# A new hand-written order for the opening of a gated-recurrence and MLP kernel, from the first unit's logarithms to the second product stage

## The chip, the cores and the metric

The kernel runs on one core of a Trainium2 chip. The metric is the time of one execution on the device, in microseconds (us). Lower is better. TensorE (PE, with its weight loads PEld), VectorE (DVE), ScalarE (ACT), GpSimd (POOL) and SyncE (SP) each run their own instructions in order, and meet through semaphores.

## The reference, cut to what matters

A linear attention with a complex, elementwise gate (4 batches, 8 heads, 768 positions, head width 48) feeds a two-layer MLP with ELU (384 to 2048 to 384). All inputs of the attention are float32; the weights arrive in the kernel as float64 bit patterns that it turns to float32 itself.

```python
mag = np.sqrt(a_re * a_re + a_im * a_im)
scale = np.minimum(mag, 0.999) / (mag + 1e-06)
a_re_n, a_im_n = (a_re * scale, a_im * scale)
for t in range(S):                      # S = 768
    ar, ai = (a_re_n[:, :, t, :, None], a_im_n[:, :, t, :, None])
    new_re = ar * S_re - ai * S_im
    new_im = ar * S_im + ai * S_re
    kv = np.einsum('bhd,bhe->bhde', k[:, :, t], v[:, :, t])
    S_re, S_im = (new_re + kv, new_im)
    y[:, :, t] = np.einsum('bhd,bhde->bhe', q[:, :, t], S_re)
...
x = y.transpose(0, 2, 1, 3).reshape(B * S, H * D)
h = x @ w_in
g = np.where(h > 0.0, h, np.exp(np.minimum(h, 0.0)) - 1.0)
return g @ w_out
```

## The kernel before, in words

The work is cut into 12 units. A unit is 128 positions of two batches, so 256 rows of the MLP. Within a unit the recurrence is done in closed form: the logarithm of the gate's size and its angle are summed over the positions by matmuls with triangular masks, and q and k are multiplied by the resulting decays and waves, so that attention becomes matmuls of "gated" q and k with a carried state.

One unit's chain, with the names of the code and the lines of the profile, is as follows.

- `squares` and `joined` (L709, L710 on ACT, L716 on DVE), and for unit 0, in smaller pieces, `squared` and `joined` (L720 on PE); then `logarithms` (L731 for unit 0, L735 and L736 later) and `powers` (L742 for unit 0, L746 and L747 later) on ACT.
- `lengths` (L766, L772), `ratios` (L757, L759, L760) and `slopes` (L780) on DVE, then `angles` (L811, L815) on ACT, an arctangent. From unit 2 on, `carried` (L826, DVE) adds the angle carried over from an earlier unit.
- `noted` (L791, ACT) notes whether the inputs lie where the fast way holds.
- `sums`, `summed`, `decayed` and `decays` (L872, L879, L920, L932, L889, L904): sums of logarithms on PE and their exponentials on ACT. `ends` (L946 to L954) takes the last of them for the state.
- `turned` and `turns` (L837 on PE, L842, L845, L849 on DVE): sums of angles, reduced to one turn. `carry_on` (L862) sends the last row on to a later unit. `waves` (L973, L976, L977, ACT): sine and cosine.
- `scaled` (L982, L986, L992) and `gated` (L1003): products of q and k with decays and waves, on DVE.
- `transposed` (L1023 on PE, L1024 a copy on ACT), `scores` (L1031, L1036) or `scored` (L1136, L1145), `states` (L1064, L1077, L1079, L1081), `values` or `valued` (L1100, L1109, with copies L1121 and L1126), and `seam` (L1190), a DMA that brings the rows of the attention into the places where the MLP reads them.

The MLP of units 0 and 1 consists of 16 `inner` and 16 `project` pieces for both units together. An `inner` (L1210) computes two blocks of 128 hidden columns for 256 rows in a PSUM bank; its `elu` uses ACT twice (L1219, L1220) and DVE once (L1221); a `project` (L1235) multiplies four such blocks by the second weight. From unit 2 on, the second layer uses sums of weight blocks (`combined`, `summed_in`, `folded`, and `product`, L1319), and from unit 3 on both layers do (L1455).

The weights come in 16 chunks, eight of each weight: `fetch` (L644) issues a chunk's DMA on SP, and `convert` does the next of the five DVE operations (L40, L43, L46, L50, L655) that make float32 of it. `load_a`, `load_qk` and `load_v` (L598) issue a unit's inputs on SP too. `warm` (L1557) issues small matmuls whose result nobody reads. `table` (L1200) loads ACT's table of functions ahead of its use. [...]three named w for the attention, three named mlp for inner products, warm matmuls and some accumulators, and y0 and y1.

The order of the opening is written by hand: the list `first` holds pieces, each with its arguments, and each engine gets its share of them in the order of the list. Units 0, 1 and 2 and the start of unit 3 are in the list. What is not in it comes from a plan of slots (`put`), sorted by time, and follows the list:

```python
items = [(fn, tuple(args)) for fn, *args in first]
items += [x[2:] for x in sorted(plan, key=lambda x: x[:2]) if x[2:] not in items]
for fn, args in items:
    fn(*args)
```

A piece moved in the list moves on every engine that it uses, and on the DMA queue.

Of the kernel before, what the change touches and what calls it, by code (L numbers as in the profile page):

```python
# [505 lines left out]
def kernel(  # L506
# [999 lines left out]
    def pronounced():  # L1506
# [13 lines left out]
        out=ident, in_=ident, pattern=[[-1, C]], base=0, channel_multiplier=1,  # L1520
# [57 lines left out]
    def gates_of(u, *at):  # L1578
# [5 lines left out]
    first = [  # L1584
        (warm, 1), (warm, 12), (fetch, "in", 0), (begun, 0), (inverses, 0), (inverses, 1),
        (load_qk, 0), (squared, "ar", 0), (load_v, 0), (squared, "ar", 1), (squared, "ai", 0),
        (joined, 0, 0), (squared, "ai", 1), (joined, 0, 1), (logarithms, 0, 0),
        (logarithms, 0, 1), (fetch, "in", 1), (fetch, "in", 2), (ratios, 0, 0), (lengths, 0, 0),
        (warm, 2), (warm, 1), (lengths, 0, 1), (sums, 1), *2 * [(convert,)],
        (table, "exp_and_others"), (ratios, 0, 1), (powers, 0, 0), (powers, 0, 1), (warm, 2),  # L1590
        (sums, 0), (warm, 1), (angles, 0, 0), (angles, 0, 1), (summed, 0), (summed, 1),
        (decayed, 0, 0), (turned, 0, 0), (decayed, 0, 1), (turned, 0, 1), (waves, 0, 0),
        (waves, 0, 1), (begun, 1), (warm, 1), (scaled, 0, "q", 0), (ends, 0), (scaled, 0, "k", 0),
        (scaled, 0, "k", 1), (scaled, 0, "q", 1), (warm, 1), (gated, 0, 0), (warm, 1), (noted, 0),
        (table, "natural_log"), (warm, 2), (gated, 0, 1), (warm, 2), *3 * [(convert,)],
        (transposed, 0, "k", 0), (transposed, 0, "q", 1), (carry_on, 0), (transposed, 0, "q", 0),
        *4 * [(convert,)], (scores, 0, 0), (transposed, 0, "k", 1), (scores, 0, 1), (load_a, 1),
        (squares, 1), (joined, 1), (fetch, "in", 3), (logarithms, 1), (states, 0, 0),
        (values, 0, 0), (powers, 1), (convert,), (states, 0, 1), (lengths, 1), (load_qk, 1),
        (convert,), (ratios, 1), (values, 0, 1), (seam, 0), (warm, 2), (warm, 2), (decays, 1),  # L1600
        (load_a, 2), (warm, 1), (inner, 0, 0), *2 * [(convert,)], (noted, 1), (scaled, 1),
        (warm, 4), (convert,), (load_v, 1), (slopes, 1), (ends, 1), *3 * [(convert,)],
        (inner, 0, 2), (elu, 0, 0), (convert,), (fetch, "in", 4), (angles, 1), (turns, 1),
        (waves, 1), (gated, 1, 0), (inner, 0, 4), (gated, 1, 1), (transposed, 1, "q", 0),
        (transposed, 1, "k", 0), (convert,), (scores, 1, 0), (load_v, 2), (convert,),
        (fetch, "in", 5), *2 * [(convert,)], (transposed, 1, "k", 1), (states, 1, 0), (convert,),
        (inner, 0, 6), (fetch, "in", 6), (elu, 0, 2), *4 * [(convert,)], (transposed, 1, "q", 1),
        (scores, 1, 1), (fetch, "in", 7), (values, 1, 0), (states, 1, 1), (values, 1, 1),
        (convert,), (seam, 1), *4 * [(convert,)], (inner, 0, 8), (inner, 0, 10), (elu, 0, 4),
        *2 * [(convert,)], (elu, 0, 6), (elu, 0, 8), (fetch, "out", 0), (warm, 2), (inner, 1, 0),  # L1610
        (convert,), (inner, 0, 12), (convert,), (inner, 1, 2), *3 * [(convert,)], (inner, 1, 4),
        (fetch, "out", 1), (fetch, "out", 2), (fetch, "out", 3), (elu, 0, 10), (convert,),
        (inner, 0, 14), (elu, 1, 0), *3 * [(convert,)], (elu, 0, 12), (fetch, "out", 4),
        *3 * [(convert,)], (elu, 1, 2), (inner, 1, 6), *2 * [(convert,)], (fetch, "out", 5),
        (elu, 1, 4), *3 * [(convert,)], (elu, 0, 14), *3 * [(convert,)], (elu, 1, 6),
        (begun, 2), (squares, 2), *2 * [(convert,)], (inner, 1, 8), (inner, 1, 10), (joined, 2),
        (convert,), (inner, 1, 12), (fetch, "out", 6), (fetch, "out", 7), *2 * [(convert,)],
        (elu, 1, 8), (convert,), (project, 0, 0, 0, 4), (convert,), (elu, 1, 10),
        *3 * [(convert,)], (elu, 1, 12), (load_qk, 2), *4 * [(convert,)], (inner, 1, 14),
        (elu, 1, 14), (logarithms, 2), (powers, 2), *4 * [(convert,)], (project, 1, 0, 0, 4),  # L1620
        (project, 1, 1, 0, 4), *3 * [(convert,)], (noted, 2), (lengths, 2), (ratios, 2),
        (slopes, 2), (load_a, 3), (angles, 2), (carried, 2), (convert,), (project, 0, 1, 0, 4),
        (convert,), (project, 0, 0, 4, 8), *3 * [(convert,)], (decays, 2), (project, 1, 0, 4, 8),
        *2 * [(convert,)], (project, 1, 1, 4, 8), (turns, 2), *2 * [(convert,)],
        (project, 0, 1, 4, 8), (begun, 3), (squares, 3), *2 * [(convert,)],
        (project, 1, 0, 8, 12), (waves, 2), (scaled, 2), (joined, 3), (gated, 2), (ends, 2),
        (load_qk, 3), (logarithms, 3), (powers, 3), (project, 1, 1, 8, 12),
        (states, 2, 0), (project, 1, 0, 12, 16), (transposed, 2, "q", 0), (lengths, 3),
        (ratios, 3), (project, 0, 0, 8, 12), (transposed, 2, "k", 0), (transposed, 2, "q", 1),
        (slopes, 3), (angles, 3), (project, 1, 1, 12, 16), (transposed, 2, "k", 1),  # L1630
        (carried, 3), (scored, 2), (turns, 3), (project, 0, 1, 8, 12), (valued, 2), (seam, 2),
        (noted, 3), (project, 0, 0, 12, 16), (opened,), (waves, 3), (summed_in, 0),
        (summed_in, 1), (combined, 1, 0), (combined, 2, 0), (summed_in, 2), (combined, 1, 1),
        (combined, 4, 0), (combined, 2, 1), (scaled, 3), (combined, 4, 1), (ends, 3),
        (project, 0, 1, 12, 16),
    ]
    def layer_of(u, at_h, at_p):
        if u == PAIRED:
# [129 lines left out]
```

## Time and profile before

| what | value |
|---|---|
| times of three runs | 670.13, 671.49, 674.26 us (median 671.49) |
| the profiled execution | 669.23 us, of which the span of the trace is 667.1 us |
| PE busy | 639.6 us (96%), weight loads 579.6 us (87%) |
| DVE busy | 503.6 us (75%) |
| ACT busy | 419.2 us (63%) |
| POOL busy | 154.4 us (23%) |
| HBM | 48.91 MB read, 4.80 MB written |

Busy time is what the profiler records between start and end of an instruction, without register, branch, semaphore and DMA-issuing instructions. "PEclk" is the clock that the throttle granted to PE, as a share of full speed. A line such as L1210 is a line of the kernel; where a wait is named, the arrow stands before the instruction that ended it.

### The profile page before, as it was taken

The numbers are of one execution on the slowest core, as the hardware profiler recorded it, in microseconds if no ns is written. First come the engines' busy times: TensorE is split into PE (matmuls) and PEld (weight loads), VectorE is DVE, ScalarE is ACT, GpSimd is POOL, SyncE is SP. The second block draws the span as 40 slices with busy tenths as digits, with TensorE's granted clock in tenths as the row PEclk, the third lists the DMA queues.
The fourth block names the chain that finished last, engine by engine and source line by source line (L and its number), as shares of the span: only waits on it lengthen the run. The fifth ranks groups of instructions, "written<-read, shape, count | busy, mean of one in ns | idle before, by whom it ended". The sixth has DMA issues, their size and how long they took to land.

```text
span 667.1 us, 17231 instructions
## 1 busy us (share of the span) xinstructions
PE 639.6 (96%) x7236; PEld 579.6 (87%) x7236; DVE 503.6 (75%) x801; ACT 419.2 (63%) x684; POOL 154.4 (23%) x200
## 2 busy tenths in 40 slices
PE   8899899999999899999999999999999999999995
PEld 6777786576898798998998998999999999999995
DVE  5889999968777788678678768768768768765481
ACT  6885455874846567667677677677677577471250
POOL 2000000112124303503503503503603602402000
PEclk9799999999999999999999999999999999999999
DMA  9986645630900632452451451451551551212100
GB/s 166 189 142 105 148 149 167 112 72 20 154 3 15 115 56 62 81 106 57 86 106 53 90 104 48 97 104 44 100 104 44 102 104 43 54 32 61 34 2 29
DMA packets 151443, 56.12 MB, mean 84 GB/s; under 512 B 129684, under 2 KB 143164, under 8 KB 151356
## 3 DMA queue, kind: packets, MB, share of 16 engines
q1 hardware_dynamic: 147616, 53.58, 38.8%
q0 software_dynamic: 3520, 1.20, 1.5%
q8 instruction: 59, 0.97, 0.6%
q14 instruction: 28, 0.23, 0.1%
q10 hardware_dynamic: 220, 0.14, 0.1%
HBM read 48.91 MB, written 4.80 MB: 81 GB/s over the span
## 4 chain that ended last, share of the span: by engine, by line
PE 44%; DVE 10%; ACT 8%; issue 3%; DMA 1%; SPq 0%; ACTq 0%; DVEq 0%
PE mlp L1319 18%; PE mlp L1455 10%; PE y L1455 5%; DVE g L1471 3%; PE w L1023 3%; DVE g L1480 3%; PE y L1109 2%; ACT ee L1477 2%; ACT ee L1476 2%; PE w L1064 2%; PE w L837 2%; DVE g L1297 1%; ACT L735 1%; DVE n L772 1%; ACT n L746 1%
## 5 line engine op out<-in xcount | busy, mean ns | idle before, releaser
L1319 PE MATMUL mlp<-w_out,g 128*128 128x192 f32 x640 | 111.8, 328 | 1.0 <-DVE ee L1331 1.0
L1319 PEld LDWEIGHTS mlp<-w_out,g 128*128 128x128 f32 x640 | 104.2, 190 | 4.4 <-DVE ee L1331 1.6
L1081 POOL TENSOR_TENSOR S<-S,T 128x384 f32<-128x384 f32 x36 | 30.9, 857 | 175.5 <-DVE S L1079 175.5
L1210 PE MATMUL mlp<-x,w_in 128*128 128x256 f32 x288 | 65.1, 381 | 3.0 <-DVE g L1221 2.6
L1210 PEld LDWEIGHTS mlp<-x,w_in 128*128 128x128 f32 x288 | 53.8, 190 | 11.7 <-DVE g L1221 3.1
L1471 DVE TENSOR_TENSOR g<-g,mlp 128x512 f32<-128x512 f32 x45 | 30.7, 682 | 40.1 <-ACT qt L1024 28.7
L1297 DVE TENSOR_TENSOR g<-g 128x512 f32<-128x512 f32 x80 | 54.4, 695 | 5.0 <-PE mlp L1319 3.8
L1455 PE MATMUL mlp<-x,w_in 128*128 128x128 f32 x424 | 56.2, 275 | 0.4 <-DVE o L1344 0.4
L1480 DVE SCALAR_TENSOR_TENSOR g<-ee,g 128x512 f32<-128x512 f32 x63 | 47.6, 755 | 11.1 <-ACT ee L1477 11.0
L1319 PE MATMUL mlp<-w,g 128*128 128x192 f32 x320 | 54.5, 329 | 0.0
L1319 PEld LDWEIGHTS mlp<-w,g 128*128 128x128 f32 x320 | 51.8, 190 | 0.6
L1455 PEld LDWEIGHTS mlp<-x,w_in 128*128 128x128 f32 x424 | 51.6, 192 | 0.8 <-DVE o L1344 0.6
L1476 ACT ACTIVATE ee<-g 128x512 f32<-128x512 f32 x63 | 39.5, 627 | 17.2 <-DVE g L1471 16.7
L1190 POOL DMA_DIRECT2D x<-y x62 | 29.8, 488 | 87.2 <-ACT y L1126 37.3
L1468 ACT COPY g<-mlp 128x512 f32<-128x512 f32 x36 | 21.1, 586 | 44.0 <-PE mlp L1455 43.7
L1477 ACT ACTIVATE ee<-ee 128x512 f32<-128x512 f32 x72 | 45.4, 631 | 2.3
L1024 ACT COPY qt<-w 128x512 f32<-128x512 f32 x48 | 25.8, 589 | 15.5 <-PE w L1023 15.4
L973 ACT ACTIVATE cs<-n 128x768 f32<-128x768 f32 (+1 forms) x14 | 10.5, 751 | 38.0 <-DVE n L845 37.9
L904 ACT ACTIVATE n<-w 64x384 f32<-64x384 f32 (+1 forms) x60 | 28.1, 486 | 8.9 <-PE w L889 8.3
L1455 PE MATMUL mlp<-x,g 128*128 128x128 f32 x224 | 29.7, 275 | 1.2 <-DVE o L1344 1.2
L1219 ACT ACTIVATE ee<-mlp 128x512 f32<-128x512 f32 x24 | 14.3, 595 | 25.6 <-PE mlp L1210 17.2
L1455 PE MATMUL y<-x,w_in 128*128 128x128 f32 x216 | 29.0, 277 | 1.4 <-ACT g L1468 1.4
(222 smaller groups left out, 1434.8 us busy)
## 6 DMA issues: line engine op xcount, KB each, us to landing
w<-in_moe_w_out_dram SPq DMA_DIRECT2D x8, 768.0 KB
g<-in_moe_w_in_dram SPq DMA_DIRECT2D x24, 256.0 KB
g<-in_moe_w_out_dram SPq DMA_DIRECT2D x24, 256.0 KB
w<-in_moe_w_in_dram SPq DMA_DIRECT2D x16, 288.0 KB
vn<-in_v_dram SPq DMA_DIRECT2D x24, 192.0 KB
ar<-in_a_re_dram SPq DMA_DIRECT2D x22, 192.0 KB
ai<-in_a_im_dram SPq DMA_DIRECT2D x22, 192.0 KB
q<-in_q_dram SPq DMA_DIRECT2D x22, 192.0 KB
```

Source lines behind the costliest of these rows:

```text
L904: nc.scalar.activation(out=flat(x[key][to, n : n + 1]), in_=t[of], func=AF.Exp, scale=sign)
L1024: nc.scalar.copy(out=o[:, h0 : h0 + 4], in_=t)
L1081: eng.tensor_tensor(out=new_s, in0=new_s, in1=wide, op=ALU.mult)
L1190: eng.dma_start(out=x["x"][ds(j * HP + D, G), i], in_=x["y"][ds(j * HP + i * G, G)])
L1210: nc.tensor.matmul(t[:, e], lhsT=w_in[:, i, ts(f + e, C)], rhs=x["x"][:, i], start=(i == 0), stop=(i == NI - 1),)
L1297: nc.vector.tensor_tensor(out=S_of(u, k, h), in0=a, in1=b, op=op)
L1319: nc.tensor.matmul(to, lhsT=a[:, m], rhs=b[:, m], start=(first and h == 0 and m == 0), stop=False, skip_group_check=True,)
L1455: nc.tensor.matmul(x["c" + c][:, ts(m, C)], lhsT=a[:, m], rhs=x["mix"][p], start=(p == BANKS[c][0] and m == 0), stop=False, skip_group_che ...
L1471: nc.vector.tensor_tensor(out=part(u, to), in0=part(u, a), in1=part(u, b), op=op)
L1476: nc.scalar.activation(out=e, in_=part(u, of), func=AF.Relu, scale=-1.0)
L1477: nc.scalar.activation(out=e, in_=e, func=AF.Exp, scale=-1.0)
L1480: nc.vector.scalar_tensor_tensor(out=part(u, to), in0=nat[u]["e", to], scalar=-1.0, in1=part(u, of), op0=ALU.add, op1=ALU.max,)
```

## The change

Only the list `first` changes. From the first unit's logarithms on it is written in another order:

- The first conversion of weights goes between unit 0's own operations, five steps in all, instead of two steps before and three after its gates. The table load for logarithms moves in between unit 0's transposes.
- The loads are permuted: `load_a(1)` goes ahead of `fetch` of chunk "in" 2, `load_qk(1)` ahead of chunk "in" 3, `load_a(3)` ahead of `load_qk(2)`, and `load_a(4)` is placed by the list, ahead of `load_v(3)`.
- Unit 0's states go ahead of its scores, its values behind them.
- Unit 1's chain (`decays`, `slopes`, `angles`, `turns`, `ends`, `scaled`) goes ahead of the first two inner pieces, (0,0) and (0,2), and unit 1's transposes, scores and states follow them. The inner pieces, their elus and the conversions after that are permuted: (0,6) ahead of (0,4), (1,8) and (0,14) ahead of (0,12) and (1,6).
- Unit 2's chain is spread among the conversions, and projects (1,0,8 to 12), (1,1,12 to 16) and (0,0,12 to 16) change places with others.
- Unit 3's `turns` goes behind the first combined sums of weights, its gates for q and for k are placed one by one, and the list goes on into unit 2's first five inner pieces and unit 4's `begun` and `squares`.
- The tables of the sine are loaded by an explicit piece for units 1, 2 and 3. The counts of warm matmuls change.

```diff
@@ -1584,55 +1584,62 @@
     first = [
         (warm, 1), (warm, 12), (fetch, "in", 0), (begun, 0), (inverses, 0), (inverses, 1),
         (load_qk, 0), (squared, "ar", 0), (load_v, 0), (squared, "ar", 1), (squared, "ai", 0),
-        (joined, 0, 0), (squared, "ai", 1), (joined, 0, 1), (logarithms, 0, 0),
-        (logarithms, 0, 1), (fetch, "in", 1), (fetch, "in", 2), (ratios, 0, 0), (lengths, 0, 0),
-        (warm, 2), (warm, 1), (lengths, 0, 1), (sums, 1), *2 * [(convert,)],
-        (table, "exp_and_others"), (ratios, 0, 1), (powers, 0, 0), (powers, 0, 1), (warm, 2),
-        (sums, 0), (warm, 1), (angles, 0, 0), (angles, 0, 1), (summed, 0), (summed, 1),
-        (decayed, 0, 0), (turned, 0, 0), (decayed, 0, 1), (turned, 0, 1), (waves, 0, 0),
-        (waves, 0, 1), (begun, 1), (warm, 1), (scaled, 0, "q", 0), (ends, 0), (scaled, 0, "k", 0),
-        (scaled, 0, "k", 1), (scaled, 0, "q", 1), (warm, 1), (gated, 0, 0), (warm, 1), (noted, 0),
-        (table, "natural_log"), (warm, 2), (gated, 0, 1), (warm, 2), *3 * [(convert,)],
-        (transposed, 0, "k", 0), (transposed, 0, "q", 1), (carry_on, 0), (transposed, 0, "q", 0),
-        *4 * [(convert,)], (scores, 0, 0), (transposed, 0, "k", 1), (scores, 0, 1), (load_a, 1),
-        (squares, 1), (joined, 1), (fetch, "in", 3), (logarithms, 1), (states, 0, 0),
-        (values, 0, 0), (powers, 1), (convert,), (states, 0, 1), (lengths, 1), (load_qk, 1),
-        (convert,), (ratios, 1), (values, 0, 1), (seam, 0), (warm, 2), (warm, 2), (decays, 1),
-        (load_a, 2), (warm, 1), (inner, 0, 0), *2 * [(convert,)], (noted, 1), (scaled, 1),
-        (warm, 4), (convert,), (load_v, 1), (slopes, 1), (ends, 1), *3 * [(convert,)],
-        (inner, 0, 2), (elu, 0, 0), (convert,), (fetch, "in", 4), (angles, 1), (turns, 1),
-        (waves, 1), (gated, 1, 0), (inner, 0, 4), (gated, 1, 1), (transposed, 1, "q", 0),
-        (transposed, 1, "k", 0), (convert,), (scores, 1, 0), (load_v, 2), (convert,),
-        (fetch, "in", 5), *2 * [(convert,)], (transposed, 1, "k", 1), (states, 1, 0), (convert,),
-        (inner, 0, 6), (fetch, "in", 6), (elu, 0, 2), *4 * [(convert,)], (transposed, 1, "q", 1),
-        (scores, 1, 1), (fetch, "in", 7), (values, 1, 0), (states, 1, 1), (values, 1, 1),
-        (convert,), (seam, 1), *4 * [(convert,)], (inner, 0, 8), (inner, 0, 10), (elu, 0, 4),
-        *2 * [(convert,)], (elu, 0, 6), (elu, 0, 8), (fetch, "out", 0), (warm, 2), (inner, 1, 0),
-        (convert,), (inner, 0, 12), (convert,), (inner, 1, 2), *3 * [(convert,)], (inner, 1, 4),
-        (fetch, "out", 1), (fetch, "out", 2), (fetch, "out", 3), (elu, 0, 10), (convert,),
-        (inner, 0, 14), (elu, 1, 0), *3 * [(convert,)], (elu, 0, 12), (fetch, "out", 4),
-        *3 * [(convert,)], (elu, 1, 2), (inner, 1, 6), *2 * [(convert,)], (fetch, "out", 5),
-        (elu, 1, 4), *3 * [(convert,)], (elu, 0, 14), *3 * [(convert,)], (elu, 1, 6),
-        (begun, 2), (squares, 2), *2 * [(convert,)], (inner, 1, 8), (inner, 1, 10), (joined, 2),
-        (convert,), (inner, 1, 12), (fetch, "out", 6), (fetch, "out", 7), *2 * [(convert,)],
-        (elu, 1, 8), (convert,), (project, 0, 0, 0, 4), (convert,), (elu, 1, 10),
-        *3 * [(convert,)], (elu, 1, 12), (load_qk, 2), *4 * [(convert,)], (inner, 1, 14),
-        (elu, 1, 14), (logarithms, 2), (powers, 2), *4 * [(convert,)], (project, 1, 0, 0, 4),
-        (project, 1, 1, 0, 4), *3 * [(convert,)], (noted, 2), (lengths, 2), (ratios, 2),
-        (slopes, 2), (load_a, 3), (angles, 2), (carried, 2), (convert,), (project, 0, 1, 0, 4),
-        (convert,), (project, 0, 0, 4, 8), *3 * [(convert,)], (decays, 2), (project, 1, 0, 4, 8),
-        *2 * [(convert,)], (project, 1, 1, 4, 8), (turns, 2), *2 * [(convert,)],
-        (project, 0, 1, 4, 8), (begun, 3), (squares, 3), *2 * [(convert,)],
-        (project, 1, 0, 8, 12), (waves, 2), (scaled, 2), (joined, 3), (gated, 2), (ends, 2),
-        (load_qk, 3), (logarithms, 3), (powers, 3), (project, 1, 1, 8, 12),
-        (states, 2, 0), (project, 1, 0, 12, 16), (transposed, 2, "q", 0), (lengths, 3),
-        (ratios, 3), (project, 0, 0, 8, 12), (transposed, 2, "k", 0), (transposed, 2, "q", 1),
-        (slopes, 3), (angles, 3), (project, 1, 1, 12, 16), (transposed, 2, "k", 1),
-        (carried, 3), (scored, 2), (turns, 3), (project, 0, 1, 8, 12), (valued, 2), (seam, 2),
-        (noted, 3), (project, 0, 0, 12, 16), (opened,), (waves, 3), (summed_in, 0),
-        (summed_in, 1), (combined, 1, 0), (combined, 2, 0), (summed_in, 2), (combined, 1, 1),
-        (combined, 4, 0), (combined, 2, 1), (scaled, 3), (combined, 4, 1), (ends, 3),
-        (project, 0, 1, 12, 16),
+        (joined, 0, 0), (squared, "ai", 1), (joined, 0, 1), (logarithms, 0, 0), (logarithms, 0, 1),
+        (fetch, "in", 1), (ratios, 0, 0), (warm, 2), (lengths, 0, 0), (convert,), (sums, 0),
+        (lengths, 0, 1), (sums, 1), (convert,), (ratios, 0, 1), (warm, 1),
+        (table, "exp_and_others"), (warm, 2), (powers, 0, 0), (powers, 0, 1), (summed, 0),
+        (convert,), (angles, 0, 0), (angles, 0, 1), (convert,), (summed, 1), (decayed, 0, 0),
+        (convert,), (turned, 0, 0), (turned, 0, 1), (decayed, 0, 1), (warm, 1), (warm, 1),
+        (begun, 1), (scaled, 0, "q", 0), (scaled, 0, "k", 1), (scaled, 0, "k", 0), (ends, 0),
+        (waves, 0, 0), (waves, 0, 1), (scaled, 0, "q", 1), (gated, 0, 0), (warm, 1), (noted, 0),
+        (warm, 1), (load_a, 1), (gated, 0, 1), (fetch, "in", 2), (transposed, 0, "q", 0),
+        (carry_on, 0), (transposed, 0, "k", 0), (table, "natural_log"), (convert,),
+        (transposed, 0, "q", 1), *2 * [(convert,)], (squares, 1), (convert,), (states, 0, 0),
+        (scores, 0, 0), (transposed, 0, "k", 1), (joined, 1), (load_qk, 1), (fetch, "in", 3),
+        (logarithms, 1), (convert,), (warm, 2), (convert,), (powers, 1), (states, 0, 1), (warm, 2),
+        (lengths, 1), (values, 0, 0), (scores, 0, 1), (warm, 2), (ratios, 1), (decays, 1),
+        (values, 0, 1), (seam, 0), (load_a, 2), (slopes, 1), (warm, 2), (angles, 1),
+        *2 * [(convert,)], (noted, 1), (scaled, 1), (ends, 1), (convert,), (load_v, 1), (warm, 1),
+        (convert,), (turns, 1), (convert,), (inner, 0, 0), (inner, 0, 2), (fetch, "in", 4),
+        (table, "trig_and_small", 1), (waves, 1), (gated, 1, 0), (gated, 1, 1), *2 * [(convert,)],
+        (transposed, 1, "q", 0), (convert,), (load_v, 2), (transposed, 1, "k", 0),
+        (transposed, 1, "q", 1), (convert,), (scores, 1, 0), (states, 1, 0), (warm, 4),
+        (fetch, "in", 5), (convert,), (elu, 0, 0), (transposed, 1, "k", 1), *2 * [(convert,)],
+        (fetch, "in", 6), (values, 1, 0), (scores, 1, 1), (convert,), (states, 1, 1), (convert,),
+        (inner, 0, 6), (elu, 0, 2), (convert,), (fetch, "in", 7), (convert,), (values, 1, 1),
+        (inner, 0, 4), (convert,), (seam, 1), (convert,), (inner, 0, 8), (convert,), (elu, 0, 6),
+        *2 * [(convert,)], (elu, 0, 4), (inner, 0, 10), (fetch, "out", 0), (elu, 0, 8),
+        *3 * [(convert,)], (warm, 2), (inner, 1, 0), (convert,), (elu, 0, 10), (inner, 1, 2),
+        (convert,), (inner, 1, 4), (convert,), (fetch, "out", 1), (convert,), (fetch, "out", 2),
+        (fetch, "out", 3), (elu, 1, 0), (convert,), (inner, 0, 14), (elu, 1, 2), *4 * [(convert,)],
+        (fetch, "out", 4), (inner, 1, 8), (inner, 0, 12), (convert,), (elu, 1, 4), (convert,),
+        (inner, 1, 6), (convert,), (fetch, "out", 5), (convert,), (elu, 1, 8), *2 * [(convert,)],
+        (elu, 0, 12), *2 * [(convert,)], (elu, 0, 14), (convert,), (begun, 2), (convert,),
+        (squares, 2), (convert,), (elu, 1, 6), (inner, 1, 10), *2 * [(convert,)], (inner, 1, 12),
+        (fetch, "out", 6), (fetch, "out", 7), (elu, 1, 10), *3 * [(convert,)], (joined, 2),
+        (convert,), (project, 0, 0, 0, 4), *3 * [(convert,)], (elu, 1, 12), *2 * [(convert,)],
+        (logarithms, 2), *2 * [(convert,)], (inner, 1, 14), (powers, 2), (convert,), (lengths, 2),
+        (elu, 1, 14), (convert,), (ratios, 2), (convert,), (slopes, 2), (project, 1, 0, 0, 4),
+        (project, 1, 1, 0, 4), *4 * [(convert,)], (noted, 2), (load_a, 3), (load_qk, 2),
+        (angles, 2), (convert,), (carried, 2), (project, 0, 1, 0, 4), *2 * [(convert,)],
+        (project, 0, 0, 4, 8), *2 * [(convert,)], (project, 1, 0, 4, 8), (decays, 2), (convert,),
+        (table, "trig_and_small", 2), (project, 1, 1, 4, 8), *2 * [(convert,)],
+        (project, 1, 0, 8, 12), (convert,), (begun, 3), (turns, 2), (squares, 3), (convert,),
+        (project, 0, 1, 4, 8), (waves, 2), (joined, 3), (ends, 2), (convert,), (scaled, 2),
+        (gated, 2), (logarithms, 3), (project, 1, 1, 8, 12), (project, 1, 1, 12, 16), (load_qk, 3),
+        (powers, 3), (project, 1, 0, 12, 16), (project, 0, 0, 8, 12), (transposed, 2, "q", 0),
+        (ratios, 3), (lengths, 3), (transposed, 2, "k", 0), (transposed, 2, "k", 1),
+        (transposed, 2, "q", 1), (slopes, 3), (table, "trig_and_small", 3), (angles, 3),
+        (project, 0, 1, 8, 12), (scored, 2), (states, 2, 0), (carried, 3), (valued, 2), (seam, 2),
+        (opened,), (noted, 3), (summed_in, 1), (summed_in, 0), (project, 0, 1, 12, 16),
+        (combined, 1, 0), (turns, 3), (waves, 3), (combined, 1, 1), (summed_in, 2),
+        (combined, 2, 0), (scaled, 3), (combined, 2, 1), (combined, 4, 0), (combined, 4, 1),
+        (ends, 3), (project, 0, 0, 12, 16), (load_a, 4), (load_v, 3), (gated, 3, None, ('q',)),
+        (inner, 2, 0), (elu, 2, 0), (gated, 3, None, ('k',)), (inner, 2, 2), (inner, 2, 4),
+        (elu, 2, 2), (elu, 2, 4), (transposed, 3, "q", 0), (summed_in, 3), (inner, 2, 6),
+        (elu, 2, 6), (folded, 2, 0, (3, 1)), (transposed, 3, "k", 0), (begun, 4), (inner, 2, 8),
+        (summed_in, 4), (elu, 2, 8), (transposed, 3, "q", 1), (squares, 4), (load_v, 4),
+        (summed_in, 5), (load_qk, 4),
     ]
     def layer_of(u, at_h, at_p):
         if u == PAIRED:
```

## The prediction

> **What bounds the kernel now.** I read the page's first two parts, then the busy times by stretch, then PE's waits in the opening, then the timelines of PE and VectorE there.
>
> ```profile
> PE 639.6 (96%) x7236; PEld 579.6 (87%) x7236; DVE 503.6 (75%) x801; ACT 419.2 (63%) x684; POOL 154.4 (23%) x200
> PE   8899899999999899999999999999999999999995
> DVE  5889999968777788678678768768768768765481
> PEclk9799999999999999999999999999999999999999
> ```
>
> TensorE is the bound, but from slice 1 to slice 7 (about 17 to 133 us) VectorE is as full. That is where the order changes. By stretches (columns: window and its length, then PE, weight loads, VectorE, ScalarE, POOL, each busy time with its count; clock, DMA share, GB/s):
>
> ```profile
> 26.00:27.00 1.00, 1.00 (x9) 1.00 (x8) 0.96 (x2) 0.73 (x2) 0.00 (x0) 0.73 1.49 199
> 27.00:28.00 1.00, 0.76 (x15) 0.52 (x15) 0.97 (x2) 1.00 (x3) 0.00 (x0) 1.00 1.30 180
> 47.00:58.00 11.00, 9.49 (x58) 7.57 (x59) 10.08 (x18) 6.40 (x11) 0.48 (x1) 1.00 0.83 143
> 58.00:84.00 26.00, 22.69 (x367) 19.69 (x363) 24.65 (x36) 12.41 (x26) 1.44 (x3) 1.00 0.63 128
> 84.00:104.00 20.00, 18.58 (x87) 16.01 (x86) 19.59 (x29) 9.97 (x16) 0.00 (x0) 1.00 0.48 157
> 104.00:128.00 24.00, 24.00 (x84) 14.46 (x85) 22.47 (x29) 16.71 (x24) 0.00 (x0) 1.00 0.72 165
> 128.00:164.00 36.00, 35.74 (x434) 24.23 (x433) 27.07 (x35) 23.01 (x37) 8.32 (x11) 1.00 0.18 38
> 300.00:400.00 100.00, 99.18 (x1256) 94.51 (x1257) 75.90 (x128) 69.83 (x112) 33.13 (x36) 1.00 0.39 83
> ```
>
> From 300 on PE is full with weight loads at 94%, and the diff leaves that order alone; so the end moves by whatever the first product of unit 2 moves (it starts at 164.1 us), plus what unit 3's opening gives or takes. Between 47 and 104 us PE is idle for 1.51+3.31+1.42 = 6.2 us. PE's own waits say for whom:
>
> ```profile
> PE mlp L1210 <- DVE g L1221: 2.6, 1, 2.6
> PE mlp L1235 <- DVE g L1221: 1.4, 1, 1.4
> PE w L1023 <- DVE qg L1003: 0.9, 1, 0.9
> ```
>
> Two of them wait for the last operation of an `elu` on VectorE, one for unit 1's gates. The timeline shows why VectorE is late:
>
> ```profile
> 12.04 0.57 DVE L40 TENSOR_SCALAR wf<-w 128x768 uint32<-128x768 uint32 x1 [1.63 <-DMA w<-in_moe_w_in_dram]
> 45.53 0.95 DVE L780 SCALAR_TENSOR_TENSOR n<-n 128x768 f32<-128x768 f32 x1
> 51.53 0.55 DVE L842 TENSOR_SCALAR n<-w 128x384 f32<-128x384 f32 x1
> 57.04 0.95 DVE L1003 TENSOR_TENSOR kg<-w,cs 128x768 f32<-128x768 f32 x1
> 127.38 0.96 DVE L655 TENSOR_TENSOR w_out<-wp,wf 128x768 f32<-128x768 f32 x1
> ```
>
> Unit 1's chain (L772, L780, ScalarE's L815, PE's L837, L842 to L849, four gates L1003) ends at 58.0, with conversions, two products and an elu between its links; the last weight chunk is converted at 128.3.
>
> [...]the clock falls in the opening: from 20 it is 0.50, at 26 it is 0.73, from 27 it is 1.00. [...]Here every wait above has ready conversions queued behind it, so order is time. [...]At 104:128 PE is 24.00 of 24.00 but loads 14.46 (60%). I do not read that as slack: the projects that run there stream 384 columns for each load (2.6 to 2.7 us for 8 records), and one follows the next without a gap.[...]
>
> **The change, part by part.** I dated the new order instruction by instruction, with the durations of this trace and each engine in its order.
>
> Start (to 30 us). The whole first conversion (L40 .56, L43 .96, L46 .56, L50 .96, L655 .95 = 4.0) now stands inside unit 0's chain; its first step, waiting for the DMA that lands at 12.04, is ahead of lengths(0,1). This makes ScalarE's powers, angles and waves about 1.0 us later and the last gate end at 25.85 instead of 24.47: +1.4. But 2.5 us of conversion that followed the gates is done. The table load in the copies (1.28 in the trace, in an idle gap at 22.91 before) now stands between them: +1.3 on the last copy. SP: unit 1's gates inputs ar/ai pass chunk in2, and q/k pass in3. At 166 to 189 GB/s of the first slices ar/ai land at about 24.4, in2 28.5, q/k 32.5; the first users are squares(1) at 30 and scaled(1) after 41, so I price this at zero, and at up to +1 if in2's conversion starves.
>
> Unit 1's chain (30 to 54 us). squares 30.0 to 31.6, L746 35.7, L772 36.7 (before 38.26): one state and the values now stand behind it. L780 ends its wait at 40.1 (before 45.53) as three conversion steps and scaled's two gates (.95 each) come after it. L815 45.0 (before 47.37), turns on PE 45.95 (before 50.48), L842 47.05 (before 51.53), last gate 54.1 (before 58.0): −3.9. Left undone at that point: one elu's L1221 (.65) and 1.6 of conversion; so VectorE's true lead is 3.9−2.2 = 1.7.
>
> Products (47 to 108 us). Inner (0,0) and (0,2), which filled PE at 41.7 and 47.8, now follow turns(1): they fill the wait for the gates, which is also the place of the 0.9 wait. Then transposes from 52.6, scores and values ahead of inner (0,6), (0,4). Inner (1,0) starts at 75.7 with the same six products behind it as at 79.08 before: PE's lead is 3.4, made of the 2.65 wait (gone, as elu (0,2) and (0,6) are earlier) and the gates' wait. The new order of inners leaves (0,14) in its bank longer, so five inners share two banks; I find waits of 0.1 each. The first project then starts at 99.4 against 103.98: −4.6, the 1.42 wait gone, because elu (1,10) and (1,12) come after more PE work.
>
> Conversions (to 128 us). The total on VectorE is the same, 16 chunks of about 4.1; out5 ends at 115.2, out6 121.9, out7 126.9 (before 128.3). Need: project (1,0,8..12) at 120.9 for out5, (1,1,12..16) at 130.1 for out7: covered by 3.2 us.
>
> Unit 2's chain. L826 is done at 123.4 and turns(2) comes at 123.5: no slack. Gates are ready at 135.3, their transposes begin at 137.9. PE work from here to unit 2's first product is the same nine projects (2.58 each), states 1.1, transposes 3.5, scored 3.0, turns 1.4, valued 3.7 = 35.9; before took 37.2 for it (127.0 to 164.2), that is 1.3 of gaps. The first product starts at 158.4 if PE is at half clock to 26.5 as now: −5.7. If unit 0's transposes run at full clock it is 157.1. In the trace, q and k transposes at 22.88 and 24.61 took 1.94 for 8 records and 2.85 for 16, against 1.05 for 8 at full clock. In the new order they come 1 to 2 us later, behind the usual end of the slow window, so I take 157.1: −7.0.
>
> Unit 3. turns(3) moves behind combined products, the gates q ahead of inner (2,0), k behind it. Its q gate is ready 7.9 us after the first product, PE reaches its transposes 7.8 after; k 10.3 against 11.3. Cost zero, each us late costs one. load_a(4) and seam(2) on POOL pass neighbours that wait for nothing near: zero. The gaps of 3.6 us at 215 to 250 stay.
>
> Sum: −7.0. The profiled execution took 669.23 (span 667.1), so 662.2; the median of the runs stands 2.26 above the profile's, so 664.5.
>
> **Rivals.**
> A, more is filled: the gaps of 47 to 104 (6.2), the .6 of warm matmuls at 78.63, and 1.3 of gaps in unit 2 all go, and 1 us of the gaps at 215: −9.1, 662.4. For it: nothing else hinders PE there. Against: VectorE's pace. An inner with elu and its share of conversions costs VectorE about 2.9 per product against PE's 2.57.
> B, the lead is given back: VectorE is full from 84 to 104 (19.59 of 20.00), elu (1,12) may end at 108.0 against 108.36, and unit 3's q gate has no slack, so PE waits where it now runs ahead. Then about −1: 670.5. Against: the conversions' need has 3.2 us of cover.
> C, slower: with the two inners out of the gap at 41 to 50, PE has only small matmuls between about 34 and 46 and the clock falls to half. The work from 47 on (two inners 5.1, transposes 3.5, scores 1.9, states 2.3, values 1.4 = 14.2) takes twice as long: +14.2, less the lead of 7.0: +7.2, 678.7. It decides from 7.0 us of such work at half clock. For it: it did happen at 20 to 26 us, with PE busy. Against: warms of 2 stand between the links, and before the clock kept 1.00 from 27 on, although PE was idle .7 and more at a time (at 38.1, before L1109).
> The change does what it says in any case: both orders are written out.
>
> **How the numbers follow.** Forecast (662.7 to 666.1 as its own range, from both clocks) 0.42; A 0.24; B 0.14; C 0.20. One per cent (6.7 us) is about what a measurement of this kernel can tell from no change: 664.8 is its lower edge. The forecast gives .26 to faster and .16 to within; A .24 faster; B .14 within; C .16 slower, and .04 within, when the half clock lasts only part. Faster 0.50, within 0.34, slower 0.16. The range takes A with 2.4 us below it, for the median's own spread (670.13 to 674.26), B, and the smaller forms of C: 660 to 675.
>
> **What would show it.** In the changed kernel's profile: L842 of unit 1 at about 47, last gate end at 54, inner (1,0) at 75 to 76, no waits of 2.6 and 1.4 for L1221, the last L655 for w_out at about 126, unit 2's first L1210 at 157 to 158, PEclk 1.00 in the slices of 33 to 67 us. A clock below 0.9 there, a wait for L1003 at unit 3's transposes, or one for L655 at a project, would make it wrong.

## The result, and the profile after

The changed kernel took 667.92 us in the median of 18 runs, the kernel before 670.23 us in 18 runs of the same session. The ratio is 0.996, with a 95% interval of 0.9948 to 0.9973: a gain of 2.3 us by the medians, less than half of the forecast 7.0 us; the time is 3.4 us above the forecast 664.5, and inside its range. The forecast had put the median 2.26 us above the profile, from three runs; by the 18 runs it stands 1.0 above. That error of 1.3 us happened to help the forecast: the gain missed by 4.7 us, not by 3.4. The profiled execution of the changed kernel took 668.01 us (span 666.1), against 669.23 (667.1) before.

The busy times of the same stretches, in the columns of the prediction (window and length; PE, weight loads, VectorE, ScalarE, POOL; clock, DMA share, GB/s), now read:

```profile
13.00:17.00 4.00, 3.94 (x11) 2.68 (x12) 3.53 (x5) 3.95 (x5) 0.00 (x0) 0.57 1.36 185
26.00:27.00 1.00, 1.00 (x6) 1.00 (x5) 1.00 (x2) 0.59 (x1) 0.00 (x0) 0.50 1.13 194
27.00:28.00 1.00, 1.00 (x7) 1.00 (x6) 1.00 (x2) 0.67 (x2) 0.00 (x0) 0.50 1.07 164
47.00:51.00 4.00, 3.88 (x10) 2.34 (x10) 3.59 (x7) 3.94 (x7) 0.00 (x0) 0.57 1.25 207
...
58.00:84.00 26.00, 24.87 (x381) 21.40 (x380) 22.31 (x33) 13.45 (x29) 1.46 (x3) 1.00 0.70 125
84.00:104.00 20.00, 20.00 (x94) 17.52 (x93) 19.52 (x28) 10.39 (x18) 0.00 (x0) 1.00 0.47 150
104.00:128.00 24.00, 24.00 (x85) 14.46 (x84) 23.48 (x31) 17.19 (x24) 0.00 (x0) 1.00 0.76 179
...
300.00:400.00 100.00, 99.19 (x1269) 94.47 (x1268) 75.64 (x128) 69.84 (x112) 32.63 (x37) 1.00 0.38 83
```

The first of these stretches in the kernel before:

```profile
13.00:17.00 4.00, 3.27 (x20) 1.80 (x19) 2.71 (x6) 3.96 (x7) 0.00 (x0) 1.00 1.42 192
```

PE has no gap left from 84 to 128 us, as forecast: the waits for L1221 are gone. But a busy PE is not a fast one here: from 13 to 17 us it is busy for 3.94 of 4.00 us, at 0.57 of its clock. The clock column is near 0.5 three times: at 13 to 17 us (0.57; 1.00 before), at 24 to 30 us (0.50; before: 0.53 at 20 to 27), and at 47 to 51 us (0.57; 1.00 before). PE's waits from 8 to 165 us name what stands ahead of each of these (waited by, waited for, us in total, times, longest):

```profile
PE w L953 <- DVE once L951: 3.0, 2, 1.7
PE mlp L872 <- DVE n L766: 2.1, 1, 2.1
PE y L1100 <- issue: 1.1, 2, 0.9
```

L766 is unit 0's second `lengths`, which now stands behind L40 on VectorE, and L40 waits 2.39 us for a DMA; L766 starts at 12.46, against 10.05 before. L951 is the small copy in the middle of `ends`; PE waits for it for 1.7 us in unit 0 and for 1.2 us in unit 1. The third wait, marked "issue", has no releaser in the trace; the last section takes it up. The timeline of both engines shows the cost at unit 0's first transposes and at unit 1's turns:

```profile
11.98 0.56 DVE L40 TENSOR_SCALAR wf<-w 128x768 uint32<-128x768 uint32 x1 [2.39 <-DMA w<-in_moe_w_in_dram]
25.09 1.94 PE L1023 MATMUL w<-ident,qg 128*128 128x128 f32 x8 [0.80 <-DVE qg L1003]
46.72 0.41 PE L953 MATMUL w<-once,pair 48*128 48x32 f32 x2 [1.24 <-DVE once L951]
47.66 2.93 PE L837 MATMUL w<-n,sum_turns 128*128 128x384 f32 x4
49.35 0.56 DVE L842 TENSOR_SCALAR n<-w 128x384 f32<-128x384 f32 x1
55.34 0.95 DVE L1003 TENSOR_TENSOR kg<-w,cs 128x768 f32<-128x768 f32 x1
129.16 0.96 DVE L655 TENSOR_TENSOR w_out<-wp,wf 128x768 f32<-128x768 f32 x1
```

The four records of L837 took 2.93 us, against 1.45 before. Unit 2's first product starts at 163.35, against 164.12 before, and from there to the end both traces run alike (unit 3's first transposes come 7.8 us after that product in both).

### The profile page after: what moved, and what is told of

It reads as the page before. It is cut to its first block, busy times and chain, and to the rows that moved or that the text cites. A ratio compares the mean times of both kernels' runs of the same rounds, so it can differ in the third digit from the quotient of the medians.

```text
span 666.1 us, 17236 instructions
## 1 busy us (share of the span) xinstructions
PE 642.1 (96%) x7236; PEld 581.4 (87%) x7236; DVE 502.2 (75%) x801; ACT 419.0 (63%) x684; POOL 154.9 (23%) x200
## 4 chain that ended last, share of the span: by engine, by line
PE 69%; DVE 12%; ACT 10%; issue 4%; SPq 3%; DMA 1%; ACTq 1%; DVEq 0%
PE mlp L1319 19%; PE mlp L1455 10%; PE mlp L1210 9%; PE w L1023 5%; PE y L1455 5%; DVE g L1471 3%; PE y L1109 3%; PE mlp L1235 3%; PE y L1235 3%; DVE g L1480 3%; PE w L1064 3%; PE w L837 3%; SPq L598 2%; ACT ee L1477 2%; ACT ee L1476 2%
## 5 line engine op out<-in xcount | busy, mean ns | idle before, releaser
L1079 DVE TENSOR_TENSOR S<-w,S 128x384 f32<-128x384 f32 x38 | 21.0, 553 | 15.2 <-POOL S L1081 10.0
```

## The experiments

Ratios are to the kernel before, on the same chip; brackets hold the 95% interval. The changed kernel stands at 0.996 [0.9948, 0.9973].

**Lengths first.** The edit puts L766 ahead of the step that waits for a DMA:

```diff
-(lengths, 0, 0), (convert,), (sums, 0), (lengths, 0, 1), (sums, 1), (convert,),
+(lengths, 0, 0), (sums, 0), (lengths, 0, 1), (convert,), (sums, 1), (convert,),
```

> The changed kernel, with unit 0's second lengths (L766) put ahead of the first conversion step (L40), which waits for a DMA until 12.0 us. Theory S (the loss against the prediction is in the start and in PE's clock: everything up to the first product shifts): PE's 2.1 us wait for L766 goes, the clock stays 1.00 at 13 to 17 us, unit 0's first gate comes at about 22 instead of 24.0, and the end is 1.5 to 2.4 us earlier than the changed kernel's: 665.5 to 666.4. Theory V (VectorE's full queue from 52 to 128 us sets the end, so that a start is worth nothing): gate at 22 too, but the end within 0.5 us of the changed kernel, 667.4 to 668.4.

Measured: 666.06 us, 0.994 [0.9924, 0.9957]. The first gate starts at 22.30 instead of 23.99, the clock at 13 to 17 us is 1.00. The profiled execution was the slowest of its 12 (669.17): PE stood still for 2.27 us at 62 us, the clock was 0.50 from 44 to 49 us, and behind that stall the 32 records of L1031 took 1.92 us, against 1.10 in the changed kernel. The median agrees with theory S; its interval touches that of the changed kernel.

**Warm matmuls in the wait.** VectorE's order stays; PE gets work.

```diff
-(convert,), (sums, 0), (lengths, 0, 1),
+(convert,), (sums, 0), (warm, 8), (lengths, 0, 1),
```

> The changed kernel, with 8 warm matmuls ahead of PE's wait for unit 0's second lengths; VectorE's order as in the changed kernel. If the idle PE of 2.1 us is what drops the clock at 13 to 17 us: L879 takes 1.46 instead of 2.01 us, the turns of unit 0 (L837) start at about 15.8 instead of 17.5, first gate at about 22.3, end 1.2 to 1.8 us earlier, 666.1 to 666.7. If the clock falls for another reason, or only the late L766 matters: L837 stays at 17 or later and the end within 0.4 us, 667.5 to 668.3.

Measured: 666.46 us, 0.9951 [0.993, 0.9973]. This is the line of 13 to 17 us in its trace:

```profile
13.00:17.00 4.00, 3.94 (x16) 2.55 (x16) 3.66 (x6) 3.94 (x6) 0.00 (x0) 1.00 1.43 191
```

L766 is as late as in the changed kernel (12.33), yet L837 starts at 15.83 instead of 17.52 and the first gate at 22.38. "Lengths first" brought that gate to 22.30, so here 1.6 of those 1.7 us come back with the clock alone. By its time this run can't be told from the changed kernel (its interval holds 0.996), and it is one trace of each.

**Warm matmuls in `ends`.** One line, between L946 and the copy L951:

```diff
+            warm(6 - u)
             once = new("once", 1, [D, NB, C // L, H])
```

> The changed kernel, with 6 (unit 0) and 5 (unit 1) warm matmuls inside ends, between L946 and L953, where PE is idle for 1.74 and 1.24 us. Theory S: the clock stays at 1.00 at 24 to 30 us and at 47 to 51 us (before: 0.50); three transposes of unit 0 take 1.05 instead of 1.93 us, unit 1's turns 1.45 instead of 2.93; states of unit 0 start about 1.9 us earlier, and the end is 2 to 3.5 us earlier, 664.4 to 665.9. Theory V: the clock does the same and the end is within 0.5 us, 667.4 to 668.4. Third: the clock falls nevertheless, since warm matmuls for 1 us are too few; then nothing moves.

Measured: 665.10 us, 0.9926 [0.9898, 0.9954]. The same two stretches:

```profile
24.00:27.00 3.00, 3.00 (x32) 2.65 (x29) 2.97 (x5) 2.69 (x6) 0.00 (x0) 1.00 0.97 141
47.00:51.00 4.00, 4.00 (x20) 3.51 (x20) 3.93 (x8) 2.76 (x5) 0.67 (x1) 1.00 1.30 193
```

Unit 1's turns start at 44.58 and take 1.56 us. The interval still touches that of the changed kernel. One caution: in this execution the clock also held at 13 to 17 us (1.00), where nothing was changed, behind a wait for L766 of 2.3 us. The mean clock over a whole execution is known for each of the six: 0.998 in four of them, as in this one, 0.992 and 0.990 in the others; all 18 of the changed kernel have 0.984 to 0.991. So the median may owe something to the same luck.

**Both repairs.**

> The edits of the first and the third together: lengths first, and warm matmuls inside ends. Theory S: the gains add, 3.5 to 6 us earlier than the changed kernel, 662 to 664.4, which is near what the prediction gave to the change. Theory V: within 0.7 us of the changed kernel, and PE waits again for VectorE between 75 and 104 us.

Measured: 664.47 us, 0.9915 [0.9886, 0.9945], clear of the changed kernel. Turns at 44.20, the first project at 99.10 (forecast 99.4), unit 2's first product at 159.44 (forecast 157.1 to 158.4). Against the changed kernel the ratios fall by 0.0020 and 0.0034 for the single repairs and by 0.0045 for both; with intervals this wide that can't be told from their sum. Theory V is out; the time lies just outside theory S's range. The clock was not fully repaired: at 24 to 27 us it was 0.63 in the profile, and two of unit 0's three transposes there took 1.94 and 1.86 us.

**Products put back.**

```diff
-(warm, 2), (angles, 1),
+(inner, 0, 0), (angles, 1),
...
-(turns, 1), (convert,), (inner, 0, 0), (inner, 0, 2),
+(inner, 0, 2), (turns, 1), (convert,),
```

> The changed kernel, with the two inner products (0,0) and (0,2) put back ahead of unit 1's turns, as in the kernel before: (0,0) ahead of unit 1's angles in place of a pair of warm matmuls, (0,2) just ahead of the turns. As the prediction had it (the chain ahead of the products gains 3 to 4 us at unit 1's gates): gates later by 2 to 3, end 1 to 3 us later than the changed kernel, 669 to 671. Theory C (PE without work loses its clock, so the gap costs as much as the earlier chain brings): the clock stays 1.00 at 47 to 51 us, turns take 1.45 instead of 2.93, and the end is within 1 us of the changed kernel on either side, 667 to 669; under 667 would make the step itself a loss.

Measured: 672.89 us, 1.0019 [1.0003, 1.0036], 4 us behind the changed kernel. But the run is not clean:

```profile
PE w L1023 <- DVE qg L1003: 3.8, 1, 3.8
PE mlp L1210 <- DMA x<-y: 3.0, 1, 3.0
```

The first product waits 3.0 us for its rows, which `seam` brings only at 46.16 in this order, and the chain waits with it. The clock was 1.00 at 47 to 51 us and the turns took 1.45 us, as theory C has it, but the fall only came a little later: right behind, from 51 to 53 us, the clock was 0.60, and product (0,2) took 4.22 us instead of 2.86:

```profile
51.86 4.22 PE L1210 MATMUL mlp<-x,w_in 128*128 128x256 f32 x12
```

Then the gates come so late that PE waits 3.8 us for them (0.9 in the kernel before). So the run supports the sign of the step, not its size: with this order of values and seam, the product could not have filled the gap at 43 to 46 us.

**Old rear.** The changed order up to inner (1,14), the order before from there on; in short:

```diff
-(inner, 1, 14), (powers, 2), (convert,), (lengths, 2), (elu, 1, 14),
+(load_qk, 2), (inner, 1, 14), (elu, 1, 14), (powers, 2), *4 * [(convert,)],
...
-(project, 1, 0, 0, 4),
+(project, 1, 0, 0, 4), (project, 1, 1, 0, 4), *3 * [(convert,)], (noted, 2), (lengths, 2),
...
```

> The changed order up to the last inner product of unit 1 (1,14), the order of the kernel before from there on (projects, unit 2's chain, unit 3's turns and gates). If the rear part is worth nothing, as priced: within 0.7 us of the changed kernel, 667.2 to 668.6. If unit 3's late turns or the permuted projects cost something: 1 to 2 us earlier, 666 to 667. If they bring what is measured: 669 to 670.

Measured: 674.07 us, 1.0044 [1.0027, 1.0061], 5.6 us behind the changed kernel (0.0084 of 670.2). No theory of mine had this. The wait that appears:

```profile
PE w L889 <- DVE n L772: 3.5, 1, 3.5
```

**Loads put back.** Chunks in2 and in3 go ahead of unit 1's inputs, as before:

```diff
-(fetch, "in", 1), (ratios, 0, 0),
+(fetch, "in", 1), (fetch, "in", 2), (ratios, 0, 0),
...
-(load_a, 1), (gated, 0, 1), (fetch, "in", 2),
+(load_a, 1), (gated, 0, 1),
...
-(load_qk, 1), (fetch, "in", 3),
+(fetch, "in", 3), (load_qk, 1),
```

> The changed kernel with only the loads of chunks in2 and in3 put back ahead of unit 1's gates and q/k. If the permuted loads are worth nothing: within 0.6 us of 667.9. If unit 1's squares are kept by ar/ai: they come later than 31.6 us and the end 1 to 2 us later, 669 to 670. If in2's late arrival starves a conversion: 1 us earlier, 667.

Measured: 667.96 us, 0.9932 [0.9908, 0.9955]. The interval touches that of the changed kernel: unclear, and repeated on a cleaner base below.

**The kernel before, with warm matmuls in `ends`.**

> The kernel before with the warm matmuls inside ends (6 and 5), nothing else. It asks what the new order is worth when PE's clock is held in both: the changed kernel with these warm matmuls took 665.1. If the order gains about 5 to 7 us at full clock: 668.5 to 670.3, for before loses its clock only at 20 to 27 us and its 2.65 and 1.42 us waits stay. If most of the gain of those warm matmuls is the clock alone, whatever the order: 665.5 to 667.5.

Measured: 671.99 us, 1.0014 [0.9995, 1.0032]: nothing, less than either expectation. The clock did rise (0.69 at 20 to 24 us, from 0.50; 1.00 at 24 to 27, from 0.58), but PE then waited 1.4 us for unit 0's gate instead of 1.0, and the 2.6 us wait for L1221 stayed. In the changed order the same line is worth 0.0034 of the time, 2.3 us; there PE has no such waits behind it. That these waits swallow the gain is a reading of the two traces; no run takes them away.

**Clean front, old rear,** and **old front, new rear.** These two complete the square.

> The front of the changed order with both repairs (lengths first, warm matmuls in ends), and the rear of the kernel before from inner (1,14) on. The changed rear with this front took 664.5, ratio 0.9915. Theory Q (the new rear is what lets VectorE keep up: with the old one unit 2's L772 stands behind conversions, and TensorE waits for it at L889): a wait of 2 to 4 us for L772 also here, though the front is early; ratio 0.995 to 0.998. Theory L (the old rear hurt in the earlier run only because VectorE was 3 us behind there): no such wait over 1 us, ratio 0.990 to 0.993.

> The opening of the kernel before up to inner (1,14), and the changed rear from there on. Theory Q: without an early front TensorE never waits for L772, so the new rear alone is worth little: 0.998 to 1.002 of the kernel before. If the rear has a gain of its own (unit 2's chain earlier, projects permuted): 0.992 to 0.996.

Measured: 669.56 us, 0.9984 [0.9969, 0.9999], just above theory Q's range, and 670.17 us, 0.9987 [0.9969, 1.0006], inside it. In the first, PE reaches unit 2's first sums (L889) early and waits:

```profile
117.56 1.30 PE L889 MATMUL w<-n,sum_logs 64*64 64x384 f32 x8 [3.52 <-DVE n L772]
118.80 6.65 PE L1236 MATMUL y<-w_out,g 128*128 128x384 f32 x16
```

The wait costs more than its 3.5 us. Behind it these sums and the two projects after them take 1.6 us longer than with the new rear (0.88 and 5.43). The old rear behind the changed front shows the same (1.27 and 6.68), and there the mean clock from 104 to 128 us was 0.93 (1.00 in the changed kernel).

Its inner (1,0) starts at 75.00, its first project at 98.39, both before those of the run with the new rear (75.72 and 99.10), and yet unit 2's first product is at 163.51 against 159.44. Theory Q holds: each half alone is worth 1 us or nothing, both with the repairs 5.7. In VectorE's timeline L772 starts at 116.56 with the old rear and at 111.62 with the new: the new list puts it ahead of six more steps of conversion and of an elu (5.0 and 0.6 us). It also puts one more project (2.7 us) ahead of L889 on PE. Which of the two moves does it was not run apart. The kernel before had no slack here: L772 ended at 119.58, and L889 started at 119.66.

**Clean order, loads back.**

> The changed order with both repairs, and the loads of in2 and in3 ahead of unit 1's gates and q/k, as before. The same loads put back in the changed order came out at ratio 0.9932 against 0.996, with intervals that touch. If the loads' order is worth nothing: 0.990 to 0.993, as without. If the old order of loads is better: 0.987 to 0.989. If unit 1's gates inputs come late: 0.994 or more.

Measured: 664.72 us, 0.9912 [0.9886, 0.9938], against 0.9915 without: the end shows no difference between the two orders. The front does: PE waits 1.55 us for unit 1's L772 in this trace, and the turns start at 46.25 instead of 44.20. Yet unit 2's first product is only 0.6 us later (160.03).

**Clean order, v for unit 2 later.**

```diff
-(load_v, 2), (transposed, 1, "k", 0),
+(transposed, 1, "k", 0),
...
-(seam, 1),
+(seam, 1), (load_v, 2),
```

> The changed order with both repairs, and the load of v for unit 2 put behind unit 1's seam, so that the transfers between 50 and 62 us are done about 1 us earlier. TensorE stands still there without a releaser for 0.9 to 2.3 us in several profiles, at records of 64 columns and fewer, just when a packet of the instruction queue is read at the end of a burst of loads. If that packet waits behind the loads: these stalls of 0.9 and more shrink by 0.5 to 1 us, and the end comes up to 1 us earlier, ratio 0.9895 to 0.991. If not: the stall stays, and the ratio is 0.991 to 0.992; a later v must not be seen, since unit 2 uses it only after 140 us.

Measured: 662.62 us, 0.9867 [0.9835, 0.9899]: the fastest, 8.8 us below the kernel before on its chip and clear of the changed kernel, but from four runs, and below both ranges that were expected. Against the run before it, on the same chip, which also has the loads put back, it is 2.1 us; those intervals touch. PE's records around 60 us, first with v early (both repairs), then with v late; L1065 is the line of `states` there:

```profile
60.84 1.01 PE L1065 MATMUL w<-vn,kg 64*64 64x48 f32 x51
62.77 0.44 PE L1065 MATMUL w<-vn,kg 64*64 64x48 f32 x13 [0.92 <-issue]
```

```profile
61.95 1.54 PE L1065 MATMUL w<-vn,kg 64*64 64x48 f32 x64
63.42 2.86 PE L1211 MATMUL mlp<-x,w_in 128*128 128x256 f32 x12
```

The stall without a releaser is gone. From unit 1's last gate to unit 2's first product the profile has 104.5 us, against 106.6 with v early. That the late v did this is not shown. In this execution the clock was 0.50 from 20 to 27 us (0.85 and 0.63 in the other), the turns start 1.8 us later (45.96), and PE reaches the place of the stall at 62.96 instead of 61.85; the last section comes back to it.

## Why the prediction was wrong, point by point

The step that failed is the start, and what PE's clock does behind it. The sum priced the start at +1.4 and then took PE at full clock for unit 0's transposes and for unit 1's turns. The runs showed +3.1, and about half of full clock in both places. Unit 2's first product came at 163.35, 6.3 us behind the 157.1 of the forecast: 4.5 up to inner (1,0), 0.3 won back up to the first project, 0.8 behind it, and 1.3 for the choice of full clock. The points below take these one by one.

- **The waits that go** were right. No wait for L1221 is left on PE, and PE is full from 84 to 128 us.
- **The start** was under-priced: +1.4 forecast, +3.1 measured (last gate of unit 0 ends at 27.55, before at 24.47). The step followed L40's DMA wait through VectorE and ScalarE, but not to PE, which stands idle for 2.1 us behind the same L766 and then runs at 0.57 of its clock: L879 took 2.01 us instead of 1.46.
- **"I take 157.1"** failed: that choice put unit 0's transposes at full clock because they come later than the slow window. The slow window moved with them. They took 1.94, 1.92 and 1.91 us, not 1.05. In this order PE waits 1.74 us for L951 just before; with warm matmuls in that wait they took 1.06, 1.06 and 1.14. With "lengths first" added the clock fell there all the same (0.63 at 24 to 27 us), so the wait alone does not decide it.
- **Unit 1's chain**: −3.9 forecast at the gates, −1.7 measured. The turns started 1.7 us later than forecast, because of the start, and then took 1.5 us more, at a clock of 0.57.
- **Products**: a lead of 3.4 us was forecast at inner (1,0); measured, it starts at 80.21, 1.1 later than before. The miss of 4.5 us adds up from the trace: turns 1.7 late, 1.5 more for the turns at half clock, 0.4 more for the two products (5.61 us), 0.9 for a stall without a releaser. From there to the first project the forecast held (23.4 us, forecast 23.7).
- **The rear** was priced at zero for the permuted projects and at "no slack" for unit 2's chain. Alone that is what it is (0.9987). What the sum left out is that PE's earlier arrival needs L772 earlier, or L889 later, as well; the new rear gives both, worth 4.6 us of the front's gain (0.9984 against 0.9915).
- **The 1.3 us of gaps** behind turns(2) were no gaps: in the kernel before, PE was busy for 35.74 of the 36 us from 128 to 164. The list of work there was too short. From the first project to unit 2's first product it was 60.1 us before and 59.8 after; the forecast had 59.0.
- **Loads and unit 3** at zero: right at the end (0.9912 against 0.9915; unit 3's transposes without a wait), though with the loads put back unit 1's turns start 2.1 us later (46.25 against 44.20). The last weight chunk was done at 130.1, not at 126.9; no project waited for it.
- **Rival C** did happen, at an eighth of its size: the clock fell at 47 us (0.57 over 47 to 51), but it was back at 51 (1.00 from 51 to 52), so that 1.9 us were lost and not 14.2. I had priced all work up to 62 us at half clock. A clock below 0.9 in these slices was among the signs that the prediction had named.

With both repairs, the ratio of 0.9915 is 5.7 us: what the sum gave with PE's slow window left as it was, and in that profile the window is still there. That the figures agree so well is partly luck: the turns start 1.8 us earlier than forecast (44.20 against 45.95), and unit 2's first product 1.0 later (159.44 against 158.4). So most of the forecast gain is in the order, and its own gaps took more than half of that back: 2.3 us are left of 5.7.

The profiled execution of the changed kernel is no odd one: its mean clock was 0.987, and all 18 have 0.984 to 0.991; the six with both repairs have 0.992 to 0.999. Which of the three places loses its clock in which execution stays open, as does the reason why it held at 13 to 17 us behind the same wait in the run with warm matmuls in `ends`.

## What to carry to other kernels

Where an order takes work out of a gap, ask what PE does in that gap. Here the clock fell to 0.50 behind waits of 1.2, 1.7 and 2.1 us with small matmuls around them. But it held at 1.00 behind a wait of 2.3 us at 11 us (warm matmuls in `ends`) and behind one of 2.65 us at 73 us (the kernel before), so these traces give no length of wait that is safe or harmful by itself. A wait on one engine has to be followed to every engine behind it, PE's clock included. And a gain at the front is worth only what the rear can take: before pricing an untouched or "neutral" rear at zero, look at which instruction of the next chain the early engine will meet first.

## What the runs showed of the hardware that I had not expected

PE stands still for 0.2 to 2.3 us with no releaser in the trace. Such stalls between 55 and 75 us fall in ten of the changed orders, at times from 58 to 71 us, but always at one of two places of the program: behind PE's 600th or 727th matmul record. In three profiles such a stall ended 1.4 to 1.6 us after the end of a transfer of 16 KB of the instruction queue, of which an execution has 59. In the changed kernel that transfer ran from 61.32 to 62.78 us and the stall of 0.91 us ended at 64.38; in "lengths first" it ran from 61.56 to 62.77 and the stall of 2.27 us ended at 64.15; with both repairs it ran from 60.02 to 61.30 and the stall of 0.92 us ended at 62.77. That PE waits there for its next instructions is a guess from these times; no run tests it.

That the instruction transfer waits behind the loads is not shown. In "lengths first" no load moved from 62 to 65 us, in the middle of the stall. And with unit 2's v late (192 KB a transfer) the transfer came at 60.36 us, no earlier than with v early (60.02); there was no stall, and PE reached its 727th record 1.1 us later, at 62.96 instead of 61.85. Whether the late v helps, and how, stays open.
